# Layer one's first block takes x from the tiles that attention filled, and the table of order is new

## The chip, the cores and the metric

The kernel runs on one core of one Trainium2 chip. The metric is device microseconds (us) of one execution, as the median of several runs. Engines have short names in the profile: PE is TensorE (matrix products; PEld its weight loads), DVE is VectorE, ACT is ScalarE, POOL is GpSimd, SP is SyncE, which here issues nearly all the DMAs (its queue is SPq). SBUF is the on-chip memory, PSUM the banks that PE writes to, DRAM the memory outside the core.

## The reference

Three parts follow each other, all in float32:

```
scores = (q @ k^T) / sqrt(64)                    # 4 batches, 8 heads, 576 tokens, 64 wide
scores = where(scores >= max(scores) - tau, scores, -1e9)
x      = softmax(scores) @ v                     # heads side by side: x is 2304 x 512
h  = x @ w_in;  g = s * relu(h)**2 + b;  x = g @ w_out           # layer one, 512 -> 2048 -> 512
h  = x @ w_in2; g = max(h,0) + alpha * min(h,0); out = g @ w_out2 # layer two, the same sizes
```

The weights come as 64-bit floats; the kernel makes float32 of them itself. Layer two forms its products by a scheme of seven products of quarters in place of eight.

## The kernel before

**Precision.** Most products are made from a high part and a low part: an operand is copied to a faster matrix format (the high part, an ACT copy), the rest is subtracted (the low part, on POOL or DVE), and three products replace one (`mm3`, L1143: lines L1144, L1145 and L1146, high with low, low with high, high with high). Only the first batch's attention works in plain float32.

**Attention.** Sixteen pairs of heads, four a batch. A pair has nine score blocks of 128 x 576 (L1421). For each score DVE takes the row maximum (L1431), POOL a threshold (L1433), ACT the exponential (L1435), and DVE masks and sums (L1437). Blocks of the exponentials are turned by PE (L920 in the fast format, L922 in plain float32, when the last of a group is not joined to the next), copied by ACT (L1550) and multiplied with v (L1563 for the first batch, L1583 later) into z, which by_sums (L1476) scales by the reciprocal sums (L1496). In the first batch a pair is done in two stages, the first 256 tokens (four scores) of all pairs ahead of the other 320 (five scores). Thus 36 scores make up the first batch.

**Splitting z.** `parts` (L1507) splits z: ACT copies the high part into a buffer (L1510), POOL or DVE subtracts (L1511) and leaves the low part in z, and two DMAs (L1514) store both in the DRAM tensor xs.

**Layer one, first half.** While attention runs, the first 1536 of the 2304 tokens go through the first part of layer one, in blocks of 256, 320, 480 and 480 (FIRST). `load_x` (L1150, DMA L1155) loads a block's four x tiles (one for each pair of heads, high and low part) from xs; `hidden` (L1161) makes one group of 128 hidden rows from the four tiles, 12 products; relu, square and split follow (`square`, L1172: ACT L1175, L1180 or L1182, ACT L1185, L1186). Ten such groups (NA = 10) are multiplied with w_out (L1702). The other six groups, and the last 768 tokens, come after attention. Until then one PSUM bank is left for hidden and for output sums in turn. The weights' conversion (L1012 to L1073: DMA, ACT, DVE and POOL) runs beside it in three staging tiles.

**What sets the order.** The code adds tasks, each with an engine (or several to choose from), a cost and a rank; a planner (Plan.run, L742) plays them against a model of the chip and lets every engine take the ready task of lowest rank whose buffers are free. MOVES (L41) is a table that adds a number to the rank of the n-th task. What comes out is a fixed instruction order for every engine; each engine works its own off in order and waits at an instruction until its inputs are there. A task that names two engines goes to the one that the planner finds free.

Of the kernel before, what the change touches and what calls it, by code (L numbers as in the profile page):

```python
# [17 lines left out]
P = 128  # L18
# [637 lines left out]
class Slots:  # L656
# [4 lines left out]
    def add(self, tiles):  # L661
        self.free.extend(tiles)
# [180 lines left out]
def tile_kernel(ctx: ExitStack, tc: tile.TileContext, q, k, v, tau, w1i, w1o, s_in, b_in, w2i, w2o, alpha, out):  # L843
# [346 lines left out]
    def square_b(h, n, r_slots, g_slots):  # L1190
# [7 lines left out]
            g.t[:, 1, :n], r.t[:, :n], f32(g.t[:, 0, :n]), op=ALU.subtract), (r, g), (g,), after=(t,), port=True)  # L1198
        return g

    SOON = -1.0


    def attention(ap):
# [843 lines left out]
```

## Time and profile before

| quantity | value |
|---|---|
| median of 3 runs | 1068.42 us (1066.39 to 1070.63) |
| profiled execution, its own time | 1068.96 us |
| its span in the profile | 1067.1 us |
| PE busy | 1043.7 us (98%) |
| DVE busy | 882.3 us (83%) |
| ACT busy | 691.9 us (65%) |
| POOL busy | 348.8 us (33%) |
| DMA | 170.87 MB, mean 160 GB/s |

The span runs from the program's first instruction to its last. A busy share is a mean over stages with different limits: attention's first batch lasts until about 115 us, attention as a whole until about 462 us, then the rest of layer one and layer two follow, with PE as the engine that is busy all the time.

### The profile page before, as it was taken

Reading aid. Unit: us, or ns where it says so; the run is one execution under the profiler, and the core shown is the slowest. Engines: PE = TensorE matmul, PEld = TensorE weight load, DVE = VectorE, ACT = ScalarE, POOL = GpSimd, SP = SyncE. Lnnn points to the kernel's source line nnn. Section 1 sums busy time; section 2 is a strip of 40 time slices with the busy share of each in tenths; the row PEclk is TensorE's granted clock in tenths of the full one; section 3 lists DMA queues with packets and bytes.
Section 4 is the critical chain, followed back from the end, with each engine's and each line's share of the span. In section 5 each row is a group of like instructions: output and inputs, shape, how many; then the busy total and the mean of one; then the engine's idle time right before and its main releaser. Section 6 shows DMA issues by size and latency. Waiting matters only on the chain.

```text
span 1067.1 us, 21196 instructions
## 1 busy us (share of the span) xinstructions
PE 1043.7 (98%) x7066; PEld 991.9 (93%) x7066; DVE 882.3 (83%) x1992; ACT 691.9 (65%) x1639; POOL 348.8 (33%) x490
## 2 busy tenths in 40 slices
PE   8889999999999999999999999999999999999998
PEld 6657899999999989989999999999999999999998
DVE  6999888888888888739867795599969999899982
ACT  6988788978877887734443463564757776556550
POOL 3677657645654476400000020110300432011110
PEclk9999999999999999999999999999999999999999
DMA  8762565666476643355585757259634564554531
GB/s 199 218 198 86 135 150 132 156 154 152 105 170 152 161 119 95 85 150 162 163 272 187 267 188 221 71 182 297 215 141 167 189 208 126 151 141 140 159 99 40
DMA packets 182188, 170.87 MB, mean 160 GB/s; under 512 B 56128, under 2 KB 160576, under 8 KB 182080
## 3 DMA queue, kind: packets, MB, share of 16 engines
q1 hardware_dynamic: 178816, 167.14, 54.4%
q10 hardware_dynamic: 3264, 2.39, 0.8%
q8 instruction: 55, 0.90, 0.4%
q14 instruction: 53, 0.43, 0.1%
HBM read 98.97 MB, written 49.28 MB: 139 GB/s over the span
## 4 chain that ended last, share of the span: by engine, by line
PE 80%; DVE 8%; ACT 5%; DMA 4%; issue 2%; SPq 1%; POOL 0%; DVEq 0%; ACTq 0%
PE bank L1144 13%; PE bank L1145 13%; PE bank L1146 12%; PE bank_b L1145 8%; PE bank_b L1144 8%; PE bank_b L1146 8%; PE sc L1421 6%; PE bank L1583 5%; PE bank L920 4%; PE bank L922 3%; DVE e L1437 1%; DMA stg<-in_moe_w_in_dram 1%; DMA stg<-in_moe_w_out_dram 1%; ACT e L1435 1%; DVE mx L1431 1%
## 5 line engine op out<-in xcount | busy, mean ns | idle before, releaser
L1437 DVE SCALAR_TENSOR_TENSOR e<-sc,mx,e 128x576 f32<-128x576 f32 x144 | 115.9, 810 | 11.9 <-ACT e L1435 8.9
L1431 DVE TENSOR_REDUCE mx<-sc 128x1 f32<-128x576 f32 x144 | 107.4, 750 | 10.6 <-PE sc L1421 9.7
L1435 ACT ACTIVATE e<-sc,mx 128x576 f32<-128x576 f32 x144 | 106.4, 743 | 11.8 <-DVE mx L1431 11.2
L1144 PE MATMUL bank<-xt,wa 128*128 128x480 f32 (+3 forms) x227 | 83.4, 368 | 0.6 <-ACT rest L1175 0.6
L1145 PE MATMUL bank<-xt,wa 128*128 128x480 f32 (+3 forms) x227 | 76.6, 337 | 0.0
L1146 PE MATMUL bank<-xt,wa 128*128 128x480 f32 (+3 forms) x227 | 76.4, 336 | 0.0
L1433 POOL TENSOR_SCALAR mx<-mx,tau_s 128x1 f32<-128x1 f32 x144 | 49.4, 344 | 77.9 <-DVE mx L1431 71.4
L922 PE MATMUL bank<-eyes_r,e 128*128 128x128 f32 (+1 forms) x244 | 70.2, 289 | 0.0
L1583 PE MATMUL bank<-gl,vt 128*128 128x256 f32 (+1 forms) x192 | 64.2, 335 | 0.0
L1583 PE MATMUL bank<-gh,vt 128*128 128x256 f32 (+1 forms) x192 | 57.8, 303 | 0.0
L1621 DVE TENSOR_TENSOR gl<-bank,gh 128x256 fp32r<-128x256 f32 (+1 forms) x96 | 43.4, 452 | 12.6 <-ACT gh L1619 11.2
L1144 PE MATMUL bank<-gt,wa 128*128 128x384 f32 (+3 forms) x144 | 51.4, 357 | 1.1 <-ACT gt L1196 0.7
L1145 PE MATMUL bank<-gt,wa 128*128 128x384 f32 (+3 forms) x144 | 49.8, 346 | 1.0 <-DVE gt L1197 1.0
L1146 PE MATMUL bank<-gt,wa 128*128 128x384 f32 (+3 forms) x144 | 49.7, 345 | 0.0
L1631 POOL TENSOR_TENSOR gr<-gf,gh 64x256 fp32r<-64x256 f32 (+1 forms) x48 | 39.1, 814 | 31.7 <-DVE gl L1629 22.3
L1619 ACT ACTIVATE gh<-bank 128x256 fp32r<-128x256 f32 (+1 forms) x96 | 39.4, 410 | 11.4 <-PE bank L922 6.4
L1144 PEld LDWEIGHTS bank<-xt,wa 128*128 128x128 f32 x227 | 43.8, 193 | 2.5 <-ACT rest L1175 1.4
L1616 POOL TENSOR_TENSOR gl<-gf,gh 128x256 fp32r<-128x256 f32 (+1 forms) x48 | 38.7, 806 | 21.7 <-ACT gh L1614 9.8
L1421 PE MATMUL sc<-k,q 128*128 128x288 f32 x200 | 43.7, 346 | 1.7 <-DMA qo<-hq 0.9
L1196 ACT ACTIVATE gt<-rest 128x384 fp32r<-128x384 f32 x56 | 29.3, 524 | 24.3 <-DVE rest L1194 23.7
L1146 PEld LDWEIGHTS bank<-xt,wa 128*128 128x128 f32 x227 | 42.6, 188 | 2.4
L1193 ACT ACTIVATE rest<-bank_b 128x384 f32<-128x384 f32 x29 | 14.2, 490 | 45.8 <-PE bank_b L1146 45.8
(832 smaller groups left out, 4214.6 us busy)
## 6 DMA issues: line engine op xcount, KB each, us to landing
stg<-in_moe_w_out_dram SPq DMA_DIRECT2D x30, 512.0 KB, 4.2
stg<-in_moe_w_in_dram SPq DMA_DIRECT2D x29, 512.0 KB, 4.1
gf<-gw SPq DMA_DIRECT2D x33, 192.0 KB, 2.5
gw<-gf SPq DMA_DIRECT2D x49, 128.0 KB, 2.9
q<-hq SPq DMA_DIRECT2D x24, 256.0 KB, 4.1
qo<-hq SPq DMA_DIRECT2D x24, 256.0 KB, 5.0
xt<-xs SPq DMA_DIRECT2D x14, 384.0 KB, 5.2
yf<-yb SPq DMA_DIRECT2D x24, 192.0 KB, 2.9
```

The lines of the kernel that those rows point to most:

```text
L920: nc.tensor.transpose(to.bitcast(F32R), part(as_r[id(x)]), one_r)
L922: nc.tensor.transpose(to, part(x), one)
L1144: nc.tensor.matmul(o, lhsT=wl, rhs=mh, start=first, stop=False, skip_group_check=on_top)
L1145: nc.tensor.matmul(o, lhsT=wh, rhs=ml, start=False, stop=False, skip_group_check=on_top)
L1146: nc.tensor.matmul(o, lhsT=wh, rhs=mh, start=False, stop=last, skip_group_check=on_top)
L1421: nc.tensor.matmul(sp.t[:, x, :HS], lhsT=o[0][:, c], rhs=o[1][:, x * HS:(x + 1) * HS], start=n == 0, stop=n == len(passes) - 1)
L1431: add("DVE", dve(S), lambda sp=sp, mx=mx: nc.vector.tensor_reduce(mx.t[:, 0:1], sp.t[:, :, :HS], op=ALU.max, axis=AX.XY, negate=True), (sp ...
L1433: t2 = add("POOL", 0.26, lambda mx=mx: nc.gpsimd.tensor_scalar(mx.t[:, 1:2], mx.t[:, 0:1], -1.0, tau_s, op0=ALU.mult, op1=ALU.subtract), ( ...
L1435: add("ACT", act(S, 1), lambda sp=sp, mx=mx, e=e: nc.scalar.activation(halves(e.t), sp.t[:, :, :HS], AF.Exp, bias=mx.t[:, 0:1]), (sp, mx), ...
L1437: add("DVE", dve(S) + 0.065, lambda sp=sp, mx=mx, e=e, col=col, sums=sums: nc.vector.scalar_tensor_tensor(halves(e.t), sp.t[:, :, :HS], mx ...
L1583: nc.tensor.matmul(o.t[:, :n], lhsT=w.rearrange("p a b -> p (a b)"), rhs=m.t[:, :n], start=c == first and x == 0, stop=c == last and x == ...
L1621: add("DVE", dve(n), lambda hi=hi, lo=lo, gt=gt: nc.vector.tensor_tensor(lo.t[:, :n], gt.t[:, :n], f32(hi.t[:, :n]), op=ALU.subtract), (gt ...
```

## The change

`parts` has a new branch for the first 256 tokens of the first batch. ACT and POOL or DVE write the high and the low part into an x tile (x0, one for each of the four pairs), and layer one's first block takes these four tiles instead of loading them. One DMA of both parts, with a late rank, still stores them in xs, because the second half of layer one reads them again. z is no longer overwritten by its low part there, and the buffer for the high part is not taken. The four x tiles are those that the following blocks load into. MOVES is a new table for all tasks. Code behind the table stands seven lines higher up to the new branch (L1144 is L1137 now, L1421 is L1415, L920 is L913) and about four lines lower behind it.

```
 MOVES = {
-    0: 30.7, 1: 30.86, 2: -2.206, 3: -2.144, 4: -22.55, 5: -12.64, 6: -14.51, 7: -54.53, 8: -677, 9: -975, 10: -768.2, 11: 17.64, 12: -521.8,
...
+    0: 2.886, 1: 10.14, 2: -6.016, 3: 25.7, 4: -24.32, 5: -10.69, 6: -32.53, 7: 25.19, 8: -144.7, 9: -90.57, 10: -68.2, 11: -51.12, 12: -213.6,
...
     SOON = -1.0
+    x0 = [Buf(x_s) for _ in range(NC)]
...
         def parts(p, to, z, rows, rank):
 
-            zh, n, t0 = Buf(r_s if p < NP else sh_s), to.stop - to.start, p // NP * S
+            n, t0 = to.stop - to.start, p // NP * S
+            if p < NP and not to.start:
+                x = x0[p]
+                t = add("ACT", act(n, 0, True), lambda: nc.scalar.activation(x.t[:, 0, :n], f32(z.t[:, to]), AF.Copy), (z,), (x,), rank=rank)
+                add([("POOL", pool2(n), rank), ("DVE", dve(n), rank + 1.0)], 0, lambda e: on(e).tensor_tensor(
+                    x.t[:, 1, :n], f32(z.t[:, to]), f32(x.t[:, 0, :n]), op=ALU.subtract), (z,), (x,), after=(t,), port=True)
+                hwdge(lambda: nc.sync.dma_start(
+                    xs[:, p * P:(p + 1) * P, to].rearrange("a p t -> p a t"), f32(x.t[:, :, :n])), (x,), rows, LATER, n, (), 4 * n, us=0.65)
+                return
+            zh = Buf(r_s if p < NP else sh_s)
...
         for j, (c0, n) in enumerate(blocks_a):
-            x = load_x(xs, of_xs(c0, n), c0, n, x_s, SOON)
+            x = load_x(xs, of_xs(c0, n), c0, n, x_s, SOON) if j else x0
```

**SP's queue at the fourth pair's first stage.** xs is the DRAM tensor, xt the x tiles, rest the buffer of the high part, stg the weights' staging, q and k the tiles of the second batch. Before:

```order
L1377 DMA k_150<-hk_152 64x576 x2
L1514 DMA xs<-rest_106 128x256
L1514 DMA xs<-z_169 128x256
L1017 DMA stg_101<-in_moe_w_out_dram 128x1024
L1155 DMA xt<-xs 128x2x256
```

After, the same place:

```order
L1371 DMA k_150<-hk_152 64x576 x2
L1010 DMA stgl<-in_moe_w_out_dram 128x1024
L1509 DMA xs<-xt 128x2x256
L1282 DMA nat_147<-in_q_dram 128x8x64
L1010 DMA stg_101<-in_moe_w_out_dram 128x1024
```

Two stores and a load have become one store; no load of a 256-column x tile is left in the program.

**PE's queue around the 24th score** (sc are the score banks, bank_120 the one bank of the hidden products, wa a weight tile). Before, the 25th and 26th scores with the fourth tile's product of the first hidden group between them:

```order
L1421 MATMUL sc_121<-k_185,gw_108 128x288 x2
L920 MATMUL bank_118<-eyes_r,e1r 128x128
L920 MATMUL bank_118<-eyes_r,e3r 128x128
L922 MATMUL bank_118<-eyes_r,e_157 128x128
L1144 MATMUL bank_120<-xt,wa_89 128x256
L1145 MATMUL bank_120<-xt,wa_89 128x256
L1146 MATMUL bank_120<-xt,wa_89 128x256
L1421 MATMUL sc_122<-k_185,gw_108 128x288 x2
```

After, from the 23rd score on:

```order
L1415 MATMUL sc_121<-k_185,gw_108 128x288 x2
L1137 MATMUL bank_120<-xt,wa_92 128x256
L1138 MATMUL bank_120<-xt,wa_92 128x256
L1139 MATMUL bank_120<-xt,wa_92 128x256
L1137 MATMUL bank_120<-xt,wa_92 128x256
L1138 MATMUL bank_120<-xt,wa_92 128x256
L1139 MATMUL bank_120<-xt,wa_92 128x256
L1137 MATMUL bank_120<-xt,wa_92 128x256
L1138 MATMUL bank_120<-xt,wa_92 128x256
L1139 MATMUL bank_120<-xt,wa_92 128x256
L913 MATMUL bank_119<-eyes_r,e5r 128x128
```

The second hidden group is under way in the new order where the old one has just three products of the first. Counted over the whole order, 84 products of the block and 171 of the transposes of L920 stand ahead of the 36th score before, 108 and 178 after.

**ACT's queue at the start** (k and gw are the first pair's key and scaled query tiles, e the exponentials). Before, from its first row behind the loading of its function table:

```order
L1347 ACTIVATE k_185<-bank_117 128x512
L1347 ACTIVATE k_185<-bank_120 128x64
L1357 ACTIVATE gw_108<-bank_120,by_half 128x64
L1357 ACTIVATE gw_108<-bank_119,by_half 128x256
L1357 ACTIVATE gw_108<-bank_117,by_half 128x256
L1435 ACTIVATE e_153<-sc_121,mx_172 128x576
```

After:

```order
L1351 ACTIVATE gw_108<-bank_118,by_half 128x256 x2
L1341 ACTIVATE k_185<-bank_119 128x512
L1341 ACTIVATE k_185<-bank_120 128x64
L1351 ACTIVATE gw_108<-bank_120,by_half 128x64
L1429 ACTIVATE e_153<-sc_121,mx_172 128x576
```

The scaling of q's first 256 columns stands ahead of k's copies now, both halves on ACT; the other scaling has moved behind the first exponential.

## Rows read from the trace of the kernel before

**Rows 1.** The page's busy time, share and instructions of each engine.
```profile
PE 1043.7 (98%) x7066; PEld 991.9 (93%) x7066; DVE 882.3 (83%) x1992; ACT 691.9 (65%) x1639; POOL 348.8 (33%) x490
```

**Rows 2.** Busy time by stretch; length, engines, PE clock, DMA share, GB/s.
```profile
12.00:40.00 28.00, 26.25 (x178) 19.25 (x179) 25.17 (x55) 25.88 (x63) 13.31 (x21) 1.00 0.86 226
40.00:65.00 25.00, 20.70 (x135) 14.51 (x133) 24.51 (x54) 22.53 (x54) 17.98 (x20) 1.00 0.80 226
65.00:85.00 20.00, 17.64 (x124) 13.32 (x124) 19.75 (x40) 18.16 (x43) 13.96 (x16) 1.00 0.54 178
85.00:109.30 24.30, 23.07 (x157) 16.89 (x155) 21.82 (x45) 20.93 (x47) 17.85 (x22) 1.00 0.19 57
109.30:130.00 20.70, 19.71 (x162) 17.23 (x161) 18.50 (x40) 16.90 (x40) 14.62 (x18) 1.00 0.56 145
130.00:800.00 670.00, 665.71 (x4298) 641.54 (x4297) 541.73 (x1172) 430.78 (x977) 215.33 (x310) 1.00 0.58 166
800.00:1067.10 267.10, 262.11 (x1978) 261.88 (x1976) 225.68 (x577) 152.09 (x411) 50.57 (x59) 1.00 0.48 142
```

**Rows 3.** Timeline, the fourth pair's x tile: start, length, engine, line, instruction.
```profile
64.34 0.41 DVE L1496 TENSOR_TENSOR z<-z,bank 128x256 f32<-128x256 f32 x1
...
65.28 0.73 POOL L1511 TENSOR_TENSOR z<-z,rest 128x256 fp32r<-128x256 f32 x1 [1.84 <-ACT rest L1510]
...
66.03 0.33 SPq L1514 DMA_DIRECT2D xs<-z  x1
...
67.82 0.37 SPq L1155 DMA_DIRECT2D xt<-xs  x1
...
72.44 0.37 PE L1144 MATMUL bank<-xt,wa 128*128 128x256 f32 x1
```

**Rows 4.** Timeline of PE, the first product of the 36th score.
```profile
109.31 0.51 PE L1421 MATMUL sc<-k,q 128*128 128x288 f32 x1
```

**Rows 5.** Instructions on the x tiles up to 109.3 us: shortest, median, longest ns.
```profile
L1144 PE MATMUL bank<-xt,wa x28: 278/365/498, 40.1 to 105.0; 128*128 128x256 f32 x28
```

**Rows 6.** Timeline of PE, a run of the block's products.
```profile
83.85 0.28 PE L1144 MATMUL bank<-xt,wa 128*128 128x256 f32 x1
...
84.20 0.28 PE L1144 MATMUL bank<-xt,wa 128*128 128x256 f32 x1
```

**Rows 7.** DVE by line and shape, 0 to 115 us: busy, mean ns, idle before.
```profile
L1431 DVE TENSOR_REDUCE mx<-sc 128x1 f32<-128x576 f32 x37 | 27.7, 751 | 4.9 <-PE sc L1421 4.6
...
L1180 DVE TENSOR_TENSOR rest<-rest 128x256 f32<-128x256 f32 x3 | 2.3, 779 | 0.2 <-ACT rest L1175 0.2
L1029 DVE TENSOR_SCALAR n<-stg 128x512 f32<-128x512 f32 x2 | 1.9, 958 | 0.0
...
L1073 DVE TENSOR_TENSOR wa<-n,wa 128x512 fp32r<-128x512 f32 x2 | 1.4, 676 | 0.0
L1355 DVE TENSOR_SCALAR gw<-bank,by_half 128x256 f32<-128x256 f32 x2 | 0.9, 472 | 0.0
L1029 DVE TENSOR_SCALAR nl<-stgl 128x512 f32<-128x512 f32 x2 | 0.8, 416 | 0.0
...
L1355 DVE TENSOR_SCALAR gw<-bank,by_half 128x512 f32<-128x512 f32 x1 | 0.8, 750 | 0.3 <-ACT gw L1357 0.3
...
L1355 DVE TENSOR_SCALAR gw<-bank,by_half 128x64 f32<-128x64 f32 x1 | 0.3, 283 | 1.6 <-ACT k L1347 1.6
```

**Rows 8.** Timeline of DVE, the two L1186 before 109 us.
```profile
102.35 1.33 DVE L1186 TENSOR_TENSOR g<-rest,g 128x256 fp32r<-128x256 f32 x1 [0.54 <-ACT g L1185]
...
108.71 0.45 DVE L1186 TENSOR_TENSOR g<-rest,g 128x256 fp32r<-128x256 f32 x1
```

**Rows 9.** Timeline of the start: k's copies and the first score.
```profile
5.90 0.71 ACT L1347 ACTIVATE k<-bank 128x512 f32<-128x512 f32 x2 [2.22 <-PE bank L922]
...
7.88 0.51 PE L1421 MATMUL sc<-k,gw 128*128 128x288 f32 x1 [0.69 <-ACT gw L1357]
```

**Rows 10.** SP's waits at the stores of z, 20 to 130 us: shortest, median, longest ns.
```profile
L1514 SPq EVENT_SEMAPHORE  x11: 17/17/1188, 27.0 to 126.1; - x11
```

1173 rows, old and new, of the table MOVES are left out of this document.

## The prediction

> **What bounds the kernel now.** I read first the busy times of the engines [rows 1], then the same by stretch [rows 2], then single instructions of the first 120 us [rows 3 to 10]. In the busy times the reader is to see TensorE (PE): busy 1043.7 of 1067.1 us. Its instructions are the same before and after, so the time can fall only where PE idles or runs thin. The stretches say where: from 12 to 130 us PE idles 1.75 + 4.30 + 2.36 + 1.23 + 0.99 = 10.6 us (length minus PE busy, [rows 2]); from 130 to 800 us only 4.3 us in 670; the 5.0 us of the last row hold the tail behind the last product. In the same rows VectorE (DVE) is busy 24.51 of 25 us (40 to 65) and 19.75 of 20 (65 to 85): in the first batch's attention DVE makes a row maximum and a masked sum for each of 36 scores, and PE has too little else to do. PE's granted clock is 1.00, the 2.4 GHz level, in every stretch, so the clock is not in play. Hence two questions: how much PE work does the change put into the thin stretch, and does it make DVE's queue longer there?
>
> **The way through memory.** It shows best at the fourth head pair, which comes last [rows 3]. The scaled result z is ready at 64.34 + 0.41 = 64.75 us; ScalarE (ACT) copies its high part, and GpSimd (POOL) has made the low part by 65.28 + 0.73 = 66.01. Then come two stores, a load issued at 67.82, and the first product with this tile at 72.44. The change removes, of this chain, the wait for the stores, the load's issue and its flight; copy and subtraction stay, with the x tile as their target. The tile is then complete at about 66.0 instead of 72.4 us: 6.4 us earlier. Each of the block's ten hidden products needs all four tiles, and one PSUM bank serves them in turn, so the block runs freely from there. SP issues four loads fewer, and four stores where there were eight; they lie off PE's path except for this chain, and I price their going at nothing beyond it.
>
> **What PE does with it.** The 6.4 us are no gain by themselves; what counts is how much work PE has behind it when the DVE-bound stretch ends, at the 36th score. Before, that score starts at 109.31 us [rows 4], and 28 triples (84 products) of the block stand ahead of it [rows 5]. In the new order 108 stand ahead of it: 24 more. One costs (84.20 − 83.85)/3 = 0.12 us in a run [rows 6], together 2.9 us. Of transposes in the fast format 178 instead of 171 stand ahead; with half the columns of a product I price one at 0.06, together 0.4 us. So PE is 3.3 us further. This work stood behind the first batch's scores before, where PE has hardly any idle time, so it counts in full if the score itself comes no later. The bounds: 0, if the added work only delays the scores that stand behind it; 6.4, the whole advance, if everything behind moves with it. I take 3.3, the count.
>
> **What DVE pays.** The new table shifts work between engines. Ahead of the 36th score's masked sum DVE now has, of query scalings (L1355), two more of 512 columns (0.75 each), three more of 64 (0.28) and one less of 256 (0.47): +1.9 us [rows 7]. It has two more L1186, at the mean of 1.33 and 0.45 [rows 8]: +1.8; one more L1073: +0.7; two fewer L1029 (mean of two forms 0.69): −1.4; one less L1180 (0.78) and one less subtraction of z (0.41, as the operation of that size in [rows 3]): −1.2 [rows 7]. Together +1.8 us. ACT loses four scalings in return, but it is not the engine that ends that stretch. With both L1186 at 0.45 the sum is +0.9; with both at 1.33 and the removed L1029 at 0.42 it is +3.3. I take the means.
>
> The two L1186 values show contention: the same operation took 1.33 us once and 0.45 us another time [rows 8]. The Trainium skill bears on it (GPSIMD Engine Reference, Specifications): GpSimd's SBUF interfaces are shared with VectorE, and a VectorE instruction with two SBUF inputs contends for them. The trace agrees as far as the spread goes. By that rule both added L1186 would meet POOL and cost 1.33, the DVE term would be +2.7 and the sum −1.2 instead of −2.1 us; by the cheaper row it would be +0.9 and −3.0.
>
> **The start.** Before, the first score (7.88 us) waits for ACT's scaling of q, which ACT does after k's copies; those run from 5.90 for 0.71 us [rows 9]. In the new order ACT scales the first q blocks before it copies k, so the first score needs k's copies alone: 6.61 us and a handover, about 6.9, if q lands early enough. I take 0.6 us earlier, with 0 and 1.0 as ends.
>
> **The sum.** −3.3 + 1.8 − 0.6 = −2.1 us. Against the profiled execution's own 1068.96 us (span 1067.1 and 1.9 around it) this is 1066.9; that execution lay 0.54 us above the median of the three runs, 1068.42, so the forecast is 1066.3 us. Past the 36th score I take the new table as neutral: PE is busy 665.71 of 670 us from 130 to 800 us [rows 2], and what is moved there stands behind work that PE has anyway. The tail keeps its form (last product, VectorE additions, store). What a changed order loses past 130 us has no cover; I give it to the rivals. A measurement of this kernel can tell 0.5% from no change, 5.3 us here: under 1063.1 is faster, over 1073.8 slower.
>
> **Rival 1, more than that.** The new table also closes waits past 130 us. For it: 4.3 us of idle time stand there [rows 2], and the whole table is new. Against it: so little in 670 us is spread over the changes of stage, where the next stage needs the first result whatever the order. If all go, −2.1 − 4.3 = −6.4, 1062.0 us; if the 6.4 us of the tile arrive in full as well, 1058.9.
>
> **Rival 2, the gain is eaten.** The change does what it says, but PE's queue is in order, and a score that comes due now stands behind up to twelve products of 0.12 us. DVE then gets its scores later and the stretch is longer by what PE does more in it. For it: DVE idles 4.6 us up to 115 us waiting for scores already [rows 7]. Against it: two score buffers lie between the two. The DVE term remains, less the start: 1068.4 + 1.8 − 0.6 = 1069.6 us.
>
> **Rival 3, slower.** SP's queue is held. Before, the store of the high part could go while the low part was being made; now the single store waits for both, and the weight and key loads behind it wait too. In the new order POOL makes three of the four low parts, among pieces of weight work. For it: SP has been held at these stores already, at most for 1.19 us [rows 10]. Against it: the first two stores now stand behind weight loads that used to come after them. If each of the four stores holds SP for 2.5 us and all of it reaches the weights that the earlier products need, 10 us of idle PE come on top: −2.1 + 10 = +7.9, 1076.3 us. It decides from (5.3 + 2.1)/4 = 1.9 us a store on.
>
> **How the numbers follow.** Forecast (1063.1 to 1068.4): 0.45. Rival 1 (under 1063.1): 0.22. Rival 2 (1068.4 to 1073.8): 0.21. Rival 3: 0.12. So faster 0.22, same 0.45 + 0.21 = 0.66, slower 0.12. The likeliest case by itself is 1065.0 to 1068.4, from −3.3 + 0.9 − 1.0 = −3.4 to −3.3 + 3.3 − 0 = 0. For 8 in 10 the range takes in rival 2 and the nearer part of rival 1: 1061 to 1073.
>
> **What would show it.** Right: no load of x until the second block; the first product with the fourth pair's tile at 65 to 67 us instead of 72.4; the 36th first-batch score at 109 to 112 us with 108 products ahead of it; PE's idle time between 65 and 130 us, 4.6 before, smaller by 2 to 3 us; that between 130 and 800 us near 4.3. It is wrong if the 36th score comes after 113 us (DVE or SP pays more), if PE waits for weight tiles between 65 and 110 us (rival 3), if the idle time from 130 to 800 us leaves 2 to 7 us, or if the first score does not come before 7.9 us.

## The result, and the profile after

The changed kernel takes 1075.46 us (median of 5 runs, 1074.63 to 1079.12), the kernel before 1069.61 in its runs beside it (5 runs, 1066.39 to 1072.35). The ratio is 1.0066, 95% interval 1.0052 to 1.0081: slower by about 7 us, where 1066.3 was forecast. The profiled execution took the median's 1075.46 us itself, with a span of 1073.7.

The page's busy times answer to [rows 1], the stretches of the windows view to [rows 2] (stretch, length, PE, PEld, DVE, ACT, POOL, the granted PE clock, DMA share, GB/s):

```profile
PE 1047.9 (98%) x7066; PEld 994.3 (93%) x7066; DVE 885.4 (82%) x1993; ACT 694.4 (65%) x1639; POOL 355.8 (33%) x489
```

```profile
12.00:40.00 28.00, 25.39 (x165) 18.98 (x165) 24.86 (x56) 23.59 (x55) 11.79 (x19) 1.00 0.78 211
40.00:65.00 25.00, 21.50 (x146) 14.88 (x146) 23.22 (x53) 22.97 (x55) 19.17 (x23) 1.00 0.63 169
65.00:85.00 20.00, 18.82 (x131) 13.94 (x126) 18.56 (x36) 17.19 (x39) 13.84 (x16) 1.00 0.60 161
85.00:109.30 24.30, 22.62 (x166) 18.56 (x165) 21.34 (x48) 22.24 (x54) 17.88 (x23) 1.00 0.40 115
109.30:130.00 20.70, 20.02 (x155) 15.84 (x153) 18.55 (x42) 17.31 (x39) 13.96 (x16) 1.00 0.35 103
130.00:800.00 670.00, 664.10 (x4273) 637.58 (x4274) 547.84 (x1174) 430.83 (x979) 221.66 (x315) 1.00 0.58 167
```

From 40 to 109 us PE is a little busier than before (62.9 us for 61.4), as forecast; from 65 to 130 us it idles 3.5 us for 4.6, which is 1.0 less where 2 to 3 less were forecast. It is not busier from 12 to 40 (25.39 for 26.25), and from 130 to 800 us, where I had taken the order as neutral, it idles 5.9 us for 4.3 and gets through 4273 matmuls for 4298. The first matmuls and the fourth pair's x tile in the changed kernel's timeline (start, length, engine, line, instruction), which answer to [rows 9] and [rows 3]:

```profile
1.20 0.45 ACTq L1282 DMA_DIRECT2D nat<-in_q_dram  x1
...
4.06 0.69 SPq L1282 DMA_DIRECT2D nat<-in_q_dram  x1
...
7.15 0.37 PE L913 MATMUL bank<-eyes_r,nat0r 128*128 128x128 f32 x1 [3.44 <-DMA nat<-in_q_dram]
...
10.03 1.90 PE L1415 MATMUL sc<-k,gw 128*128 128x288 f32 x4
...
68.13 0.42 DVE L1507 TENSOR_TENSOR xt<-z,xt 128x256 fp32r<-128x256 f32 x1
...
69.15 0.36 PE L1137 MATMUL bank<-xt,wa 128*128 128x256 f32 x1
```

The first score starts at 10.03 us, 2.15 later than before, where 0.6 earlier was forecast: PE stood idle for 3.44 us until a load of q landed. The x tile does what it was to do: complete at 68.55, used at 69.15, which is 3.3 us earlier than before, though not within the forecast 65 to 67. Two stretches are left to explain, the first 12 us and what follows 130.

**A count used below.** PE's busy time hides short gaps. So I also count, up to a time, PE's time less what its matmuls take in an undisturbed run of the traces: columns at 2.4 a nanosecond plus 13 to 19 ns each (the run in [rows 6] comes to 10), and 58 and 87 ns for the two kinds of transposes. It is an estimate, worked out from each trace's matmul starts: its absolute values hang on these costs, while the differences between kernels move by at most some 0.5 us with other costs. A difference between two kernels is PE time lost (in e2 and e11 some 1.7 us of it to a fall of the clock between 56 and 62 us).

| PE time not covered, us, up to | 20 | 118 | 150 | 310 | 470 | end |
|---|---|---|---|---|---|---|
| before | 12.1 | 46.7 | 48.2 | 55.7 | 60.0 | 62.4 |
| changed | 14.0 | 47.9 | 50.7 | 61.5 | 67.0 | 68.5 |
| e1, old order | 12.9 | 47.6 | 49.6 | 56.0 | 60.8 | 62.2 |
| e2, old start, then new | 11.8 | 46.2 | 48.9 | 58.9 | 64.2 | 66.1 |
| e9, new start, then old | 14.1 | 50.0 | 51.9 | 57.8 | 62.4 | 64.3 |
| e11, new from 12 to 305 | 12.7 | 46.3 | 49.2 | 59.7 | 68.4 | 71.0 |
| e12, new from 305 | 12.8 | 47.9 | 49.6 | 55.6 | 61.7 | 64.0 |

Of the 6.1 us at the end the changed kernel has lost 1.9 by 20 us; at 118 us only 1.2 of them are left, and from there to 310 it loses 4.6 more (13.6 for 9.0). From 150 to 310 us the count grows by 10.0 to 10.8 us in the three kernels that have the new order there (changed, e2, e11), and by 5.9 to 7.5 in the four that have the old one.

### The profile page after: what moved, and what is told of

It reads as the page before. It is cut to its first block, busy times and chain, and to the rows that moved or that the text cites. A ratio compares the mean times of both kernels' runs of the same rounds, so it can differ in the third digit from the quotient of the medians.

```text
span 1073.7 us, 21176 instructions
## 1 busy us (share of the span) xinstructions
PE 1047.9 (98%) x7066; PEld 994.3 (93%) x7066; DVE 885.4 (82%) x1993; ACT 694.4 (65%) x1639; POOL 355.8 (33%) x489
## 4 chain that ended last, share of the span: by engine, by line
PE 80%; DVE 9%; ACT 6%; DMA 3%; issue 2%; SPq 0%; POOL 0%; DVEq 0%; ACTq 0%; POOLq 0%
PE bank L1137 12%; PE bank L1138 12%; PE bank L1139 12%; PE bank_b L1138 8%; PE bank_b L1137 8%; PE bank_b L1139 8%; PE sc L1415 6%; PE bank L1587 5%; PE bank L913 4%; PE bank L915 3%; DMA stg<-in_moe_w_out_dram 2%; ACT e L1429 1%; DVE e L1431 1%; DVE mx L1425 1%; PE bank L1567 1%
## 5 line engine op out<-in xcount | busy, mean ns | idle before, releaser
L1137 PE MATMUL bank<-xt,wa 128*128 128x480 f32 (+3 forms) x227 | 82.9, 365 | 1.9 <-ACT rest L1168 1.8
L1427 POOL TENSOR_SCALAR mx<-mx,tau_s 128x1 f32<-128x1 f32 x144 | 49.2, 343 | 68.0 <-DVE mx L1425 58.7
L1186 ACT ACTIVATE rest<-bank 128x384 f32<-128x384 f32 x36 | 17.7, 492 | 54.3 <-PE bank L1139 54.1
L1137 PE MATMUL bank<-gt,wa 128*128 128x384 f32 (+3 forms) x142 | 50.5, 356 | 0.3 <-DVE yb L1906 0.3
L1138 PE MATMUL bank<-gt,wa 128*128 128x384 f32 (+3 forms) x142 | 48.8, 344 | 0.0
L1139 PE MATMUL bank<-gt,wa 128*128 128x384 f32 (+3 forms) x142 | 48.7, 343 | 0.0
L1137 PEld LDWEIGHTS bank<-xt,wa 128*128 128x128 f32 x227 | 43.6, 192 | 5.0 <-ACT rest L1168 2.9
L1115 POOL TENSOR_TENSOR wa<-stg,wa 128x256 fp32r<-128x256 f32 x8 | 8.2, 1030 | 111.1 <-ACT wa L1114 111.1
L1190 DVE TENSOR_TENSOR gt<-rest,gt 128x384 fp32r<-128x384 f32 x55 | 33.3, 606 | 13.0 <-ACT gt L1189 12.8
```

What stands on the lines that cost most here:

```text
L1137: nc.tensor.matmul(o, lhsT=wl, rhs=mh, start=first, stop=False, skip_group_check=on_top)
L1138: nc.tensor.matmul(o, lhsT=wh, rhs=ml, start=False, stop=False, skip_group_check=on_top)
L1139: nc.tensor.matmul(o, lhsT=wh, rhs=mh, start=False, stop=last, skip_group_check=on_top)
L1427: t2 = add("POOL", 0.26, lambda mx=mx: nc.gpsimd.tensor_scalar(mx.t[:, 1:2], mx.t[:, 0:1], -1.0, tau_s, op0=ALU.mult, op1=ALU.subtract), ( ...
```

## The experiments

The change is two: tiles that are filled directly, and another order. To part them, most of these kernels replace the planner's choice by a written list of (task, engine) in the sequence in which the planner of one kernel or the other issued them:

```
-        t.ways = [(e, u, (r + MOVES.get(n, 0), n)) for e, u, r in ways]   # run(): best rank first
+        for w in ORDER.split(): ...                                       # run(): as listed, each engine in turn
```

Two lists can be joined at a time of the plan: the one's tasks up to there, then the other's without those already done. All have the direct tiles. The lists (B is that of before, C that of the changed kernel, the number the time of the joint in us):

```
e1  ORDER = B                  e2  ORDER = B, 12, C            e3  ORDER = B, 118, C
e4  ORDER = C, 118, B          e6  ORDER = B, 455, C           e7  ORDER = C, 455, B
e8  ORDER = B, 150, C, 455, B  e9  ORDER = C, 12, B
e11 ORDER = B, 12, C, 305, B   e12 ORDER = B, 305, C
```

**e1, the old order throughout.** PE's instructions are those of before, one by one; on SP, for each of the four pairs:

```
-DMA xs<-rest 128x256
-DMA xs<-z 128x256
+DMA xs<-xt 128x2x256
 ...
-DMA xt<-xs 128x2x256
```

> The kernel before with one thing of the change: the attention's high and low parts go into the x tiles, one store for both, the four loads gone. Every instruction else stands on its engine where it stood before; none of the new order. Theory A (the direct tiles are harmless and the new order costs the time): 0 to 2 us below the kernel before, ratio 0.998 to 1.000, since TensorE's order still puts the first block's products where they were. Theory B (the direct tiles themselves cost, by the store that waits for both parts and holds SP): about 5 us above it, ratio 1.004 to 1.006.

Measured: 1069.33 us, ratio 1.0004 (0.9994 to 1.0014). Theory B falls: the direct tiles and the single store cost nothing, and in the old order they bring nothing. Its fourth tile is complete at 67.45 us, but the first product with it stands where it stood in PE's queue and starts at 73.88.

**e2, the old order for the first 12 us, then the new.**

> The changed kernel, with the order of before for the first 12 us alone (k before q; 10 rows of TensorE, 3 of VectorE, 14 of SP differ), the new order from there. Theory A1 (the first score, 2.2 us later after the change, is a loss that stays to the end): 2 us below the changed kernel, about 1073.4, ratio to the kernel before 1.0035. Rival (the late start is made up by the thin stretch to 130 us): as the changed kernel, ratio 1.0055. If it comes out at the kernel before (1.000), the start is the whole cause.

Measured: 1073.62, ratio 1.0039 (1.0025 to 1.0054). The start is a loss that stays, but not the whole.

**e3 and e4, the two orders joined at 118 us.**

> The changed kernel's direct tiles, in the order of before up to about the 40th score (some 118 us), and in the new order from there to the end. Theory A2 (most of the loss is many short waits of TensorE between 130 and 470 us, which the new order makes): ratio 1.004 to 1.006, about 1074.5. Rival (the loss is made ahead of 118 us, and what follows only carries it): ratio 0.999 to 1.001.

> The mirror: direct tiles, the new order up to about the 40th score (some 118 us) and the order of before from there. Theory A2: the loss of the new order up to 130 us alone, 1.2 us by the two traces, so ratio 1.001 (0.999 to 1.002). Rival (loss ahead of 118 us): ratio 1.005. The two halves together should give the changed kernel's 5.9 us if the halves don't act on each other.

Measured: 1.0085 (1.0070 to 1.0099) and 1.0074 (1.0058 to 1.0090). Both miss every theory, and together they exceed the whole loss: the joint itself costs. The windows of e4 around it show how:

```profile
118.00:136.20 18.20, 13.82 (x108) 11.32 (x106) 12.71 (x30) 11.75 (x26) 8.75 (x12) 1.00 0.27 81
136.20:143.00 6.80, 6.02 (x29) 5.61 (x30) 4.01 (x9) 4.14 (x11) 3.01 (x3) 0.50 0.78 184
143.00:150.00 7.00, 7.00 (x64) 7.00 (x63) 5.81 (x15) 6.03 (x16) 3.65 (x6) 1.00 0.65 165
```

PE idles 4.4 us behind the joint, and then its granted clock falls to 0.50, the 1.2 GHz level, for 6.8 us, in which PE does 29 matmuls where the next 7.0 us hold 64. e3's trace has the like: PE busy for 12.20 us of 15.9 from 118 us on, and then the clock at 0.50 from 133.9 to 137.3. As a test of where the loss lies these two are inconclusive.

**e5, one load behind the transposes.** The changed kernel with one row of SP moved; the other engines' rows are the same.

```
 L1269 DMA nat_145<-in_k_dram 64x2x64
 L1282 DMA nat_147<-in_k_dram 128x8x64
-L1282 DMA nat_143<-in_q_dram 128x2x64
 L1274 DMA v_188<-in_v_dram 128x2x256
-L1282 DMA nat_143<-in_q_dram 128x2x64
+L1282 DMA nat_143<-in_q_dram 128x2x64 x2
```

> The changed kernel with one instruction moved: the load of q's third and fourth block (one of its two halves) is issued after the transposes of the first two blocks instead of ahead of them; the order on the other four engines is the same word for word. Theory S1 (those transposes, the first work of TensorE on data, wait for that load though they don't read it): they start at about 4.5 us instead of 7.15, the first score comes at 8 us or before instead of 10.03, and the time falls by 1 to 3 us, ratio to the kernel before 1.004 to 1.006. Rival S2 (they wait for their own two halves, which land late since four loads share the DMA engines): they start within 0.5 us of 7.15, the time stays, ratio 1.0066.

Measured: 1075.41, ratio 1.0070 (1.0057 to 1.0083). PE's rows of this kernel's timeline:

```profile
4.43 0.34 PE L913 MATMUL bank<-eyes_r,nat0r 128*128 128x128 f32 x1 [0.73 <-DMA nat<-in_q_dram]
...
8.28 2.13 PE L1415 MATMUL sc<-k,gw 128*128 128x288 f32 x4
...
10.63 2.04 PE L1415 MATMUL sc<-k,gw 128*128 128x288 f32 x4
...
14.88 1.24 PE L1415 MATMUL sc<-k,gw 128*128 128x288 f32 x4 [0.24 <-DVE e L1431]
```

S1's mechanism is shown: the transposes of q's first two blocks had waited for a load that they don't read, the one issued at 4.06 us (in the changed kernel it landed at 7.10, their own two loads by 4.28), and start at 4.43 now. Its price is not: the first two scores take 2.13 and 2.04 us instead of some 1.2, as PE's matmuls are still slow there (see the last section), and two scalings of q's later blocks (0.47 us on ACT, 0.48 on DVE), which in the old order lie ahead of the first maximum, come between the maxima and the masked sums. The third score starts at 14.88, in the changed kernel at 15.34, before at 11.89. What the load would be worth with the matmuls at full speed this run doesn't show. That the start's order as a whole costs time is shown by e2 and e9.

**e6, e7 and e8, joints at 455 and 150 us.** At 455 us the attention is nearly over, and the two orders have done the same but five tasks.

> Direct tiles, the order of before through the whole attention (to about 455 us, where the two orders have done the same tasks but five loads), then the new order. Theory A2: ratio 0.999 to 1.002, the second half of the new order costs nothing. Rival (the new order also loses past 455 us, as the idle time at 740 to 800 us suggests): ratio 1.002 to 1.004.

> The mirror: direct tiles, the new order through the whole attention (to about 455 us), then the order of before. Theory A2: the loss is all there, ratio 1.005 to 1.007. Rival: ratio 1.002 to 1.004, the rest being lost past 455 us.

> Direct tiles, the order of before to about 150 us and from 455 us on; between the two the new order alone. In the cut at 118 us the joint itself cost TensorE 3 to 8 us; at 150 us the two orders differ in 19 tasks done instead of 29, so less. Theory A2 (the new order's handovers between 150 and 455 us are the larger part of the loss): 4 us above the kernel before plus the joint, ratio 1.004 to 1.007, and in the waits between 150 and 470 us more of the kind 'transposes wait for VectorE's gl' and 'scores wait for VectorE's e' than in the run with the old order. Rival (those waits came from the late start, not from the order there): ratio 0.999 to 1.002 and waits as in the kernel before.

Measured: 0.9999 (0.9990 to 1.0008), 1.0075 (1.0063 to 1.0087) and 1.0076 (1.0062 to 1.0089). Past 455 us the new order costs nothing; the loss is all ahead of it. e8 lies above its bound of 1.007: its count grows by 17.2 us from 150 to 470 (11.2 in e1), as theory A2 has it, but a joint and 3.4 us at clock 0.50 behind 489 us are in its time.

**e9, the new order for the first 12 us alone**, the mirror of e2.

> The mirror of the second run: direct tiles, the new order for the first 12 us alone, the order of before from there (at that cut the two orders differ in two tasks done). Theory A1 (the start, q before k, costs the time that the second run gave back): 2 to 3 us above the run with the old order throughout, ratio 1.002 to 1.003; the first score at about 10 us, the 36th 2 to 3 us later than with the old start. Rival (the thin stretch makes the start up): ratio 0.999 to 1.001.

Measured: 1071.10, ratio 1.0022 (1.0011 to 1.0033). The first score starts at 10.27 us. The 36th in e1, in e9 and in the changed kernel:

```profile
110.75 0.51 PE L1415 MATMUL sc<-k,q 128*128 128x288 f32 x1
```

```profile
113.15 0.51 PE L1415 MATMUL sc<-k,q 128*128 128x288 f32 x1
```

```profile
114.83 0.41 PE L1415 MATMUL sc<-k,q 128*128 128x288 f32 x1
```

The start costs 2.4 us by the traces of e9 and e1, 1.9 by their ratios, and 2.9 by the ratios of e2 and the changed kernel.

**e10, an empty table** in the changed kernel, with its planner:

```
-MOVES = {0: 2.886, 1: 10.14, ...}
+MOVES = {}
```

> The changed kernel with an empty table: the planner's own rules alone set the order. It tells how much of the time such a table holds, and so what scale a new draw of it moves on. If the table is worth little (rival), the ratio is within 1.000 to 1.010 and 6 us between two tables would be much; if it is worth tens of microseconds, as I expect (1.02 to 1.05), two tables that differ by 6 us agree to a fifth of their worth, and any change that needs a new table carries a loss or gain of this size with it.

Measured: 1082.68, ratio 1.0136 (1.0115 to 1.0157). Less than I expected and more than the rival: against no table the old one is worth some 14 us (the direct tiles being neutral, by e1) and the new one some 7, so the 7 us between the two orders are as much as the new table is worth at all.

**e11 and e12, the new order from 12 to 305 us, and from 305 on.**

> Direct tiles, the order of before up to 12 us and from 305 us on (there the two orders differ in 11 tasks done, all of them ahead in the new one), the new order between. By the second run's trace, read against the first run's, the new order loses some 3 us of TensorE's time between 150 and 310 us and nothing net before that. If that reading is right (theory A3): ratio 1.002 to 1.004. If the loss is not of that stretch but of the later attention (rival): 0.999 to 1.001.

> The mirror: direct tiles, the order of before up to 305 us, the new order from there. Theory A3: what is left of the loss, about 1 us, between 310 and 455 us; ratio 1.000 to 1.002. Rival: 1.003 to 1.005. Both runs above 1.003 would mean that the joint at 305 us itself costs.

Measured: 1.0055 (1.0042 to 1.0067) and 1.0011 (1.0002 to 1.0020). The second is as theory A3 has it and the rival is out. The first is above its bound of 1.004: in the count it loses 3.7 us to e1 by 310 us, as e2 does (2.9), and 3.5 more from there to 350, behind the joint, where the windows show the clock at 0.50 again:

```profile
310.00:320.70 10.70, 8.06 (x54) 7.18 (x53) 6.72 (x17) 6.29 (x15) 3.22 (x6) 1.00 0.97 221
320.70:324.10 3.40, 3.40 (x18) 3.40 (x19) 1.66 (x4) 1.37 (x4) 0.65 (x2) 0.50 0.01 5
324.10:330.00 5.90, 5.90 (x42) 5.52 (x41) 4.50 (x10) 3.84 (x8) 1.97 (x4) 1.00 0.12 42
```

**Where PE waits from 150 to 310 us.** PE's waits there (what waited, for what: us in total, times, longest), in the changed kernel, in e2, in e1 and in the kernel before:

```profile
PE bank L913 <- DVE gl L1625: 1.0, 2, 0.7
PE bank L1137 <- ACT rest L1168: 1.0, 3, 0.4
PE sc L1415 <- DVE e L1431: 0.7, 1, 0.7
PE sc L1415 <- issue: 0.3, 1, 0.3
PE bank L913 <- DVE z L1648: 0.2, 1, 0.2
```

```profile
PE bank L913 <- DVE gl L1625: 1.0, 2, 0.7
PE bank L1137 <- ACT rest L1168: 1.0, 3, 0.4
PE sc L1415 <- DVE e L1431: 0.7, 1, 0.7
PE bank L913 <- DVE z L1648: 0.2, 1, 0.2
```

```profile
PE bank L913 <- DVE gl L1633: 0.2, 1, 0.2
PE sc L1415 <- DMA q<-hq: 0.2, 1, 0.2
```

```profile
PE sc L1421 <- DMA qo<-hq: 0.9, 1, 0.9
PE bank L920 <- DVE gl L1629: 0.2, 1, 0.2
```

In the kernels with the new order there these are the same seven waits, 2.9 us, early start or late (the changed kernel has one more, of 0.3); with the old order they are 0.4 in e1 and 1.1 before. By the count the changed kernel loses 4.4 us to e1 in this stretch; these waits make 2.8 of it, and where the rest goes is not shown. Behind 190 us e8 has them too, whose order ahead of 150 us is the old one: they are not work given back that had been brought ahead. One of them in e2's timeline:

```profile
279.00 0.44 ACT L1623 ACTIVATE gh<-bank 128x320 fp32r<-128x320 f32 x1
279.09 0.38 PE L1139 MATMUL bank<-xt,wa 128*128 128x480 f32 x1
...
279.30 0.22 PE L913 MATMUL bank<-eyes_r,e2r 128*128 128x128 f32 x1
...
279.43 0.30 PE L915 MATMUL bank<-eyes_r,e 128*128 128x128 f32 x1
279.50 0.57 ACT L1168 ACTIVATE rest<-bank 128x480 f32<-128x480 f32 x1
...
280.13 0.49 PE L1137 MATMUL bank<-xt,wa 128*128 128x480 f32 x1 [0.41 <-ACT rest L1168]
```

One PSUM bank serves the hidden blocks in turn. The last product of one is issued at 279.09, ACT clears the bank from 279.50 to 280.07, and the next block's first product stands three transposes behind, 0.3 us of work: PE waits. The other kinds are alike: a transpose waits for the bank that DVE's `gl` reads, a score for the bank of the masked sum.

## Why the prediction was wrong

**What bounds the kernel, and the way through memory: right.** In e2, which starts as before, the fourth tile is complete at 65.22 + 0.66 = 65.88 us and used at 66.53, as the prediction had it (66.0; 65 to 67), 5.9 us earlier than in [rows 3]; e1 shows that the direct tiles alone bring nothing.

```profile
65.22 0.66 DVE L1507 TENSOR_TENSOR xt<-z,xt 128x256 fp32r<-128x256 f32 x1
...
66.53 0.36 PE L1137 MATMUL bank<-xt,wa 128*128 128x256 f32 x1
```

**What PE does with it: right. What DVE pays: right in size by luck, for another reason.** e9 and the changed kernel start alike and part at 12 us. Their windows from there to the 36th score, at 113.15 and 114.83 us (e9, then the changed kernel):

```profile
12.00:113.15 101.15, 90.94 (x610) 66.52 (x609) 93.84 (x196) 89.61 (x207) 64.03 (x80) 1.00 0.56 160
```

```profile
12.00:114.83 102.83, 93.86 (x638) 69.97 (x637) 93.09 (x200) 90.57 (x211) 66.96 (x83) 1.00 0.59 162
```

and, of the same stretches, DVE's wait for scores:

```profile
DVE mx L1425 <- PE sc L1415: 5.0, 7, 1.8
```

```profile
DVE mx L1425 <- PE sc L1415: 6.6, 10, 1.6
```

The changed kernel has 108 products ahead of that score for 84, and PE did 2.9 us more (3.3 forecast). The score came 1.7 us later (1.8 forecast), though not by DVE's work, which fell by 0.8 us (and by 1.5 against the kernel before, 94.92 us up to that score for 96.44). The sum had the added operations right and their prices wrong: of the four L1179 (L1186 before) ahead of the 36th masked sum three took 0.41 to 0.42 us and one 1.03, where each added one stood at 0.89; two of the three L1066 (L1073 before) took 1.76 and 1.77, where 0.7 stood; and others got shorter, as the four TENSOR_SCALAR e<-e,rc with 2.1 us for 3.6. DVE waited 1.6 us longer for scores: at the longest of these waits past the first score, 1.16 us at 92.35, the score stands behind twelve products, as Rival 2 has it. What is left is 1.2 us by these windows and 2.1 at 118 us by the count, against −3.3 + 1.8 = −1.5.

**The start: the first step that failed, with the wrong sign.** −0.6 us was forecast, "if q lands early enough"; it cost 2.4 (e9). I had the condition and did not price its failure: the transposes wait for a third load of the same tile, and the first sums for scalings that had been made earlier. Without that wait the first score starts at 8.28 (e5), still not at 6.9.

**Neutral past the 36th score: the second, and the larger.** I argued that PE is 99% busy there and what is moved stands behind work that PE has anyway. The windows from 118 to 310 us, of e1 and of the changed kernel:

```profile
118.00:310.00 192.00, 190.80 (x1457) 180.93 (x1456) 170.13 (x400) 160.02 (x377) 115.83 (x172) 1.00 0.61 148
```

```profile
118.00:310.00 192.00, 187.61 (x1420) 176.47 (x1419) 168.52 (x394) 158.58 (x373) 114.45 (x171) 1.00 0.57 141
```

PE idles 3.2 us longer and does 37 matmuls less. From 118 us to the end the count grows by 20.6 us in the changed kernel, by 14.6 in e1 and 15.7 before: 5 to 6 us where I had put 0, two thirds or more of them between 150 and 310 us, where the waits shown above are the part that can be seen. The text gave what a changed order loses there "to the rivals", but no rival held it. The sign that was to show it did not: the idle time from 130 to 800 us is 5.9 us, within the 2 to 7 that counted as neutral.

**Rival 3**, slower by SP's stores, named about the measured time, 1076.3, for a reason that did not act; that its number is near is luck. SP was held at the merged stores for longer than the 1.9 us from which it was to decide, in the changed kernel at each of the four (2.0 to 4.3 us), in e1 at three (2.7 to 4.7). SP's waits, 20 to 130 us, in the changed kernel, then in e1:

```profile
SPq L1509 <- POOL mx L1427: 7.6, 2, 4.3
SPq L1509 <- POOL xt L1507: 3.0, 1, 3.0
SPq L1509 <- DVE n L1026: 2.0, 1, 2.0
```

```profile
SPq L1509 <- POOL xt L1507: 5.5, 2, 2.8
SPq L1509 <- DVE xt L1507: 4.7, 1, 4.7
```

Nothing came of it: e1, held for 10.2 us in all, takes the time of the kernel before, between 20 and 118 us the changed kernel gains on e9, and between 65 and 110 us none of its PE waits is for a weight tile. The 1.19 us of [rows 10] are the length of the longest semaphore instruction and not all of SP's waiting; by the view used here SP was held at the stores of z before the change too, for up to 3.5 us.

So against e1 the sum is −2.1 in the thin stretch, + 2.4 of the start, + 6.0 behind: +6.3 us of PE's time, beside some 6 to 7 us measured. The direct tiles by themselves are worth nothing here. What stays open is why the new order is tight at just these handovers: an order that fills them was not tried. None of these kernels beats the one before; e1 and e6 equal it.

## What to carry to other kernels

When a change of code comes with a new order, part the two: the old order with the new code told more here than any reading of the trace. "The engine is full there" is no proof that an order is neutral; its waits by kind, in a stretch of some 150 us, show in pieces of 0.2 to 0.7 us what a busy share of 99% hides. And a change of order at the start is priced with its condition failed as well: in e9 what the start lost was not made up later (2.4 us behind e1 at 118 us, 2.1 at the end).

## What the runs showed of the hardware

The granted clock fell to 0.50 in the midst of a run, in e4 behind 18.2 us with PE busy for 13.82, in e3 behind 15.9 with 12.20, in e11 behind 10.7 with 8.06, in e8 behind 9.1 with 7.34, and in the thin stretch, between 56 and 65 us, in e2, e4, e10 and e11. The matmuls of such a stretch come at about half the pace (29 in 6.8 us and 64 in the next 7.0 in e4), so a rearranged order can cost more than its idle time.

The clock's entries in the trace begin at 4.6 us in the kernel before and 5.1 in e2, at 11.6 in the changed kernel, and between 8.9 and 13.3 in the others; e1 has the same PE instructions as before, the same gap (PE idle from 4.55 to 5.28; before 4.56 to 5.30), and its first entry at 10.7. Ahead of the first entry the windows' clock column reads 1.00, yet there the matmuls of a score take 687 ns each for 406 behind it. So that column says nothing of the first microseconds, and a first score took 1.24 us before and 2.29 in e1, with the same order of PE ahead of it.
